# Attention products as tiles of TensorE's array: scores on alternating row groups, po and pi in two halves of their output columns

## The chip, the cores and the metric

One core of one Trainium2 chip runs the program. The metric is the device time of one execution in microseconds (us), lower is better. Engines: PE is TensorE (a matmul is a weight load, listed under PEld, and a streaming part, listed under PE), DVE is VectorE, ACT is ScalarE, POOL is GpSimd, SP issues DMAs.

## The reference, cut to what matters

Three stages in a row: a gated linear attention (a recurrence over 768 steps for each of 4 x 8 heads of size 40), a feed-forward layer, and a layer of 8 experts of which each token takes one.

```python
C = f_stab[:, :, None, None] * C + i_stab[:, :, None, None] * np.einsum('bhd,bhe->bhde', vt, kt)
n = f_stab[:, :, None] * n + i_stab[:, :, None] * kt
h_tilde = np.einsum('bhde,bhe->bhd', C, qt)
nq = np.einsum('bhd,bhd->bh', n, qt)[:, :, None]
y[:, :, t] = o * h_tilde / np.maximum(np.abs(nq), 1.0)
...
h = x @ w_in                 # 3072 x 320 by 320 x 2048
x = (h - np.tanh(h)) @ w_out
...
h = np.maximum(x[mask] @ w1[e], 0.0)
out[mask] = gate_w[mask, None] * (h @ w2[e])
```

## The kernel before, in words

The recurrence is worked in 6 chunks of 128 time steps. A **unit** is one chunk of one batch entry, 8 heads together, so there are 24 units (4 in each chunk). The q and k of a unit lie transposed in SBUF with two heads in one column of 128 partitions: even heads in partitions 0 to 39, odd heads in 64 to 103. All attention matmuls have fp32 operands, and the trace holds two records (a weight load and a matmul each) for one of them.

A unit's work is a list of small functions in `unit`:

- `scores(par)` (S) makes the products of k and q for the four heads of one parity into one PSUM bank `ps`, 4 matmuls with 40 rows of weights, 128 columns of weights and 128 streamed columns (line 517). Then ACT takes the exponentials of the decay tile `D` (line 521) and POOL masks it (line 522).
- `weigh(par)` (W): DVE multiplies `ps` by `D` into `A` (line 533), which frees the bank.
- `outs` (O): `po` is the carried state `Cst` under q, 4 matmuls of 104 x 128 weights and 82 streamed columns (line 541, not in chunk 0); `st`, in the same bank, is the new state, 8 matmuls with 40 columns of weights, at output partitions 0 and 64 in turn (line 545, not in the last chunk); `pi` is `A` times v, 8 matmuls of 128 x 128 weights and 41 streamed columns (line 548).
- `sums`, `finish` (M, F): DVE joins `po` and `pi`, normalises, and updates the state. `turn` (U) transposes the result into `px` (line 597), `low` (L) writes it as the two halves `xh` and `xl` of the feed-forward layer's input (lines 602 and 604).

The feed-forward layer runs in 6 x 16 steps, one for each chunk and each 128 columns of `w_in`. A step issues `gemm1` of three steps ahead (8 matmuls of 512 streamed columns into `h`, line 183), ACT and DVE work on `h` (lines 207 to 216 and 160), and `gemm2` of this step (12 matmuls of 320 streamed columns, lines 191 to 193). It works on chunk c while the attention of chunk c+1 is slotted between its steps: unit b of a chunk has its `scores(0)` in step 4b - 4, counted from the start of the chunk whose layer is being worked, and `scores(1)` one step later. `PLACE1` and `PLACE2` give each function its step offset and its slot, `ORDER` is the order of the slots in a step. The attention of chunk 0 and of the first unit of chunk 1 stands in a list written out by hand, `START`, and goes before. A scheduler may move an instruction ahead of one that stands earlier and isn't ready. After step 96 come the experts (80 steps of the same kind, lines 183 and 191 to 193 again), with no attention beside them.

From `START` on, PSUM banks for the attention come from `at_bank`: in `START` out of 7 banks in turn, later out of the two banks of the pool `at`, which `ps`, `po`, `pi` and `px` share.

Of the kernel before, what the change touches and what calls it, by code (L numbers as in the profile page):

```python
# [21 lines left out]
L = 128  # L22
# [86 lines left out]
def build(ctx, tc, qk, vk, og, gat, w64, w12, emb, tau, cst, tok, empty, out):  # L109
    nc = tc.nc  # L110
    V, A, G, T = nc.vector, nc.scalar, nc.gpsimd, nc.tensor
    MM = T.matmul
# [31 lines left out]
    def at_bank(name):  # L144

        if wide:
            pool, tag = wide[0]
            wide.append(wide.pop(0))
            return pool.tile([128, 512], F32, tag=tag, name=name)
        return at_p.tile([128, 512], F32, tag="at", name=name)  # L150
# [222 lines left out]
    Cst = attp.tile([104, 16, 82], F32, tag="C", name="C", bufs=1)  # L373
# [16 lines left out]
    def load_d(i):  # L390

        if i < NCH * B:
            c, b = divmod(i, B)
            for par in range(2):
                r0 = (8 * b + 4 * par) * L
                src = gd[min(c, 1)][max(c - 1, 0), r0:r0 + 4 * L].partition_broadcast(128)
                if c:
                    t = attp.tile([128, 4, L], F32, tag="D", name="D", bufs=4)
                else:
                    t = wpool.tile([128, 4, L], F32, tag="wi", name="D")  # L400
                nc.sync.dma_start(out=t.rearrange("p h t -> p (h t)"), in_=src)
                Dg[i, par] = t
# [7 lines left out]
    def load_unit(i, early=False):  # L410

        if early:
            a = []
            for tag, src in (("wi", qk[i, :, 0:512]), ("wi", qk[i, :, 512:1024]), ("wo", vk[i, :, 0:328]), ("wo", vk[i, :, 328:648])):
                t = wpool.tile([128, src.shape[1]], F32, tag=tag, name="ue")
                nc.sync.dma_start(out=t, in_=src)
                a.append(t)
        else:
            t = attp.tile([128, 1024], F32, tag="W", name="W")
            nc.sync.dma_start(out=t, in_=qk[i])  # L420
            a = [t[:, 0:512], t[:, 512:1024]] + load_vk(i)
        units[i] = a
# [75 lines left out]
    def attention(c):  # L498
# [3 lines left out]
        def unit(b):  # L502
            i = c * B + b
            uq, uk, uv, ukk = units.pop(i)
            qT = uq.rearrange("p (j t) -> p j t", j=4)
            kT = uk.rearrange("p (j t) -> p j t", j=4)
            v1 = uv.rearrange("p (h d) -> p h d", h=8)
            kk = ukk.rearrange("p (h d) -> p h d", h=8)
            v = {}

            def scores(par):
                p0 = 64 * par
                ps = v['ps', par] = at_bank("ps")
                warm(ps)
                for j in range(4):
                    sl = slice(j * L, (j + 1) * L)
                    MM(ps[:, sl], kT[p0:p0 + 40, j, :], qT[p0:p0 + 40, j, :], start=True, stop=True)
                Dt = v['D', par] = Dg.pop((i, par))
                for j in range(4):
                    k = 8 * i + 4 * par + j  # L520
                    A.activation(out=Dt[:, j, :], in_=Dt[:, j, :], func=AF.Exp, bias=bcol[:, k:k + 1])  # L521
                G.affine_select(out=Dt, in_=Dt, pattern=[[0, 4], [1, L]], compare_op=ALU.is_ge, fill=0.0,  # L522
                                base=0, channel_multiplier=-1)
# [12 lines left out]
            def outs():  # L536
                po = v['po'] = at_bank("po")
                st = po[:, 336:500].rearrange("p (j d) -> p j d", j=4)
                if c:
                    for j in range(4):  # L540
                        MM(po[:, 82 * j:82 * j + 82], qT[0:104, j, :], Cst[:, 4 * b + j, :], start=True, stop=True)
                if c + 1 < NCH:
                    for h in range(8):
                        p0 = 64 * (h % 2)
                        MM(st[p0:p0 + 40, h // 2, :], v['kw'][:, h, :], v1[:, h, :], start=True, stop=True)
                pi = v['pi'] = at_bank("pi")
                for h in range(8):
                    MM(pi[:, 41 * h:41 * h + 41], v['A', h % 2][:, h // 2, :], v1[:, h, :], start=True, stop=True)
                if i >= 4:
                    load_d(i + 2)  # L550
                if 4 <= i < NCH * B - 2:
                    load_unit(i + 2)
# [46 lines left out]
            def low():  # L599
# [7 lines left out]
                nc.sync.dma_start(out=ys[i * 128:(i + 1) * 128, :], in_=v['y'][:, 0:320])  # L607

            return scores, weigh, outs, sums, finish, turn, low

        us = {}
# [113 lines left out]
    def warm(bank, n=None):  # L725
        for _ in range((WARM if c0[0] else 0) if n is None else n):
            MM(bank, oneb, busy, start=True, stop=True)
# [146 lines left out]
    def step(n):  # L874

        if n < NS:
            return n // NF, n % NF, None
        p, f = divmod(n - NS, NFE)
        return p, f, PASSES[p]
# [56 lines left out]
    for n in range(NS + NE):  # L936
        c, f, ps = step(n)
# [73 lines left out]
    def first(w, xt):  # L1011
        h = at_bank("h")
        for k in range(3):
            n = min(128, 320 - 128 * k)
            MM(h[:, 0:128], w[0:n, 128 * k:128 * k + 128], xt[0:n, k, :], start=k == 0, stop=k == 2)
        return h
# [6 lines left out]
    with tc.If(reg > CAP):  # L1023
# [5 lines left out]
        with tc.If(reg > 4096):  # L1029
# [7 lines left out]
            with tc.For_i(0, NT, 128) as i:  # L1037
# [4 lines left out]
                with tc.For_i(0, DFF, 128) as f:  # L1042
# [10 lines left out]
                    h = first(wf, xt)[:, 0:128]  # L1053
# [27 lines left out]
        for e in range(E):  # L1081
            tiles = nc.values_load(nti[0:1, e:e + 1], min_val=0, max_val=NT // 128)
            V.tensor_copy(out=off, in_=st[:, e:e + 1])
            with tc.For_i(0, tiles):
# [11 lines left out]
                for f in range(NFE):  # L1096
                    nc.sync.dma_start(out=wf, in_=w12[e * NFE + f])
                    h = first(wf, xt)[:, 0:128]
# [70 lines left out]
```

## Time and profile before

| | |
|---|---|
| median of 3 runs | 798.19 us (793.8, 798.33, 798.19) |
| the profiled execution | 794.33 us, its span 792.6 us |
| mean granted clock of TensorE | 0.959 |
| PE, PEld busy | 756.1 us (95%), 672.6 us (85%) |
| DVE, ACT, POOL busy | 572.8 us (72%), 448.9 us (57%), 175.2 us (22%) |
| DMA | 98.51 MB, mean 124 GB/s |

The span is the time from the first to the last instruction; 1.7 us of the execution lie outside it. Busy times are of the whole span, and the stages have different limits, so the shares are read by stage. A row of the timeline merges neighbouring instructions of one kind: "x8" is eight of them, the time beside it is from the first one's start to the last one's end, and a matmul's end is modelled.

### The profile page before, as it was taken

To read this page: it belongs to the slowest core of one execution; us is meant where nothing else is said; L and a number is where in the kernel's file an instruction comes from. 1 tells how busy PE (TensorE), PEld (TensorE's weight loads), DVE (VectorE), ACT (ScalarE), POOL (GpSimd) and SP (SyncE) were. 2 spreads that over 40 slices of the span, in tenths; PEclk is the share of its full clock that TensorE was granted. 3 is DMA by queue.
4 is the path that set the end of the run, shared out by engine and by line. 5 is a ranking of instruction groups with operands and counts; after the bars stand their busy time and mean duration, and the time that the engine had idled before them with its cause. 6 is when DMAs were issued, how large, how long until landed. Compare 5 with 4: busy or idle time off the path is not lost. (4 is left out here: it accounts for less than half of the span.)

```text
span 792.6 us, 13944 instructions
## 1 busy us (share of the span) xinstructions
PE 756.1 (95%) x4768; PEld 672.6 (85%) x4768; DVE 572.8 (72%) x1464; ACT 448.9 (57%) x1079; POOL 175.2 (22%) x231
## 2 busy tenths in 40 slices
PE   8979998999999999999999999798999999999993
PEld 4758787788888888888888888687999999999993
DVE  5385899889886988699768877995747765556310
ACT  3686687684457555754567445765636645546321
POOL 2292265411131112111211011302031102102111
PEclk8557999999999999999999999999999999999998
DMA  7665777522242223322251102014265745535000
GB/s 253 230 202 214 257 255 262 160 81 76 69 149 77 79 71 112 112 79 79 70 153 50 40 34 91 1 55 149 98 209 152 226 148 172 146 126 164 25 22 22
DMA packets 47281, 98.51 MB, mean 124 GB/s; under 512 B 13278, under 2 KB 21641, under 8 KB 46544
## 3 DMA queue, kind: packets, MB, share of 16 engines
q1 hardware_dynamic: 44496, 89.44, 35.6%
q0 software_dynamic: 2512, 7.89, 2.6%
q8 instruction: 39, 0.64, 0.3%
q14 instruction: 42, 0.34, 0.1%
q10 hardware_dynamic: 192, 0.20, 0.1%
HBM read 85.57 MB, written 17.87 MB: 131 GB/s over the span
## 5 line engine op out<-in xcount | busy, mean ns | idle before, releaser
L183 PE MATMUL h<-xh,wi 128*128 128x512 f32 (+6 forms) x880 | 295.0, 372 | 6.8 <-ACT xh L847 2.6
L191 PE MATMUL acc<-wo,ghi 128*128 128x320 f32 (+1 forms) x616 | 197.4, 321 | 6.1 <-ACT ghi L215 4.2
L183 PEld LDWEIGHTS h<-xh,wi 128*128 128x128 f32 x880 | 164.6, 190 | 33.7 <-DVE glo L160 4.5
L183 PE MATMUL h<-xl,wi 128*128 128x512 f32 (+6 forms) x528 | 190.9, 366 | 0.0
L192 PE MATMUL acc<-wo,ghi 128*128 128x320 f32 (+1 forms) x616 | 190.5, 310 | 0.0
L193 PE MATMUL acc<-wo,glo 128*128 128x320 f32 (+1 forms) x616 | 185.4, 311 | 0.0
L191 PEld LDWEIGHTS acc<-wo,ghi 128*128 128x128 f32 (+1 forms) x616 | 114.7, 186 | 11.6 <-ACT ghi L215 6.9
L192 PEld LDWEIGHTS acc<-wo,ghi 128*128 128x128 f32 (+1 forms) x616 | 114.7, 186 | 2.8
L193 PEld LDWEIGHTS acc<-wo,glo 128*128 128x128 f32 (+1 forms) x616 | 113.3, 185 | 2.5
L183 PEld LDWEIGHTS h<-xl,wi 128*128 128x128 f32 x528 | 100.7, 191 | 10.0
L215 ACT ACTIVATE ghi<-h 128x512 fp32r<-128x512 f32 x96 | 56.8, 591 | 76.0 <-DVE h L210 42.7
L207 ACT ACTIVATE u<-h 128x512 f32<-128x512 f32 x96 | 57.1, 595 | 72.8 <-PE h L183 70.3
L870 DVE SCALAR_TENSOR_TENSOR glo<-h,ghi 128x256 fp32r<-128x256 f32 (+5 forms) x80 | 41.4, 517 | 60.6 <-ACT ghi L869 53.7
L521 ACT ACTIVATE D<-D,bcol 128x128 f32<-128x128 f32 x192 | 63.5, 391 | 32.3 <-DMA D<-gd 28.5
L209 DVE SCALAR_TENSOR_TENSOR s<-s,u 128x512 f32<-128x512 f32 x96 | 69.4, 723 | 16.2 <-ACT s L208 15.6
L522 POOL TENSOR_SCALAR_AFFINE_SELECT D<-D 128x512 f32<-128x512 f32 x48 | 34.5, 719 | 209.3 <-ACT D L521 158.0
L160 DVE TENSOR_TENSOR glo<-h,ghi 128x512 fp32r<-128x512 f32 x96 | 66.1, 689 | 19.0 <-ACT ghi L215 14.9
L260 DVE SCALAR_TENSOR_TENSOR jk<-R,enb 128x320 bf16<-128x320 f32 x152 | 77.1, 508 | 3.0 <-ACT R L668 2.8
L869 ACT ACTIVATE ghi<-h 128x256 fp32r<-128x256 f32 (+5 forms) x80 | 36.7, 459 | 66.9 <-PE acc L192 59.7
L208 ACT ACTIVATE s<-u,cs 128x512 f32<-128x512 f32 x96 | 69.2, 721 | 1.1
L160 DVE TENSOR_TENSOR wi<-ew,wi 128x256 fp32r<-128x256 f32 (+1 forms) x128 | 46.1, 360 | 28.7 <-ACT wi L172 27.3
L210 DVE SCALAR_TENSOR_TENSOR h<-s,h 128x512 f32<-128x512 f32 x96 | 66.1, 689 | 0.6
(180 smaller groups left out, 1017.4 us busy)
## 6 DMA issues: line engine op xcount, KB each, us to landing
ew<-in_w SPq DMA_DIRECT2D x64, 352.0 KB
D<-gd SPq DMA_DIRECT2D x48, 256.0 KB
raw<-in_w SPq DMA_DIRECT2D x16, 704.0 KB
W<-in_qk SPq DMA_DIRECT2D x20, 512.0 KB
vk<-in_vk SPq DMA_DIRECT2D x20, 324.0 KB
xs<-blank SPq DMA_DIRECT2D x32, 161.0 KB
sg<-in_og SPq DMA_DIRECT2D x6, 640.0 KB
ys<-y SPq DMA_DIRECT2D x24, 160.0 KB
```

Of the source, the lines that this page charges most:

```text
L160: eng.tensor_tensor(out=out, in0=x, in1=hi.bitcast(F32), op=ALU.subtract)
L183: MM(h[:, 0:cols], wi[:, k, :], x[:, kk, :], start=n == 0, stop=n == len(seq) - 1)
L191: MM(o, ghi[:, sl], wo[:, 0, 0:320], start=first, stop=False)
L192: MM(o, ghi[:, sl], wo[:, 1, 0:320], start=False, stop=False)
L193: MM(o, glo[:, sl], wo[:, 0, 0:320], start=False, stop=last)
L207: A.activation(out=u, in_=h, func=AF.Square, accum_out=usum[:, n:n + 1])
L208: A.activation(out=s, in_=u, func=AF.Square, bias=col(C_BETA))
L209: V.scalar_tensor_tensor(out=s, in0=s, scalar=GAMMA, in1=u, op0=ALU.add, op1=ALU.mult)
L210: V.scalar_tensor_tensor(out=h, in0=s, scalar=C2, in1=h, op0=ALU.mult, op1=ALU.mult)
L215: A.activation(out=ghi, in_=g, func=AF.Copy)
L260: V.scalar_tensor_tensor(out=jk[1], in0=x2, scalar=1.0, in1=enb[:, e, :], op0=ALU.mult, op1=ALU.mult, accum_out=lg[:, j, e:e + 1])
L521: A.activation(out=Dt[:, j, :], in_=Dt[:, j, :], func=AF.Exp, bias=bcol[:, k:k + 1])
```

## The change

`scores(0)` now makes the matmuls of both parities: it takes two banks, and goes over j with the even head (partitions 0 to 39) into one bank and the odd head (partitions 64 to 103) into the other in turn. `scores(1)` keeps only its exponentials and mask. Each matmul for `po` and for `pi` becomes two, with columns 0 to 63 and 64 to 127 of the weights, which write output partitions 0 to 63 and 64 to 127; each streams the same 82 or 41 columns as before. `st` stays as it is.

```diff
             def scores(par):
-                p0 = 64 * par
-                ps = v['ps', par] = at_bank("ps")
-                warm(ps)
-                for j in range(4):
-                    sl = slice(j * L, (j + 1) * L)
-                    MM(ps[:, sl], kT[p0:p0 + 40, j, :], qT[p0:p0 + 40, j, :], start=True, stop=True)
+                if par == 0:
+                    for p in range(2):
+                        v['ps', p] = at_bank("ps")
+                        warm(v['ps', p])
+                    for j in range(4):
+                        sl = slice(j * L, (j + 1) * L)
+                        for p in range(2):
+                            r = slice(64 * p, 64 * p + 40)
+                            MM(v['ps', p][:, sl], kT[r, j, :], qT[r, j, :], start=True, stop=True)
...
                 if c:
                     for j in range(4):
-                        MM(po[:, 82 * j:82 * j + 82], qT[0:104, j, :], Cst[:, 4 * b + j, :], start=True, stop=True)
+                        for p0 in (0, 64):
+                            MM(po[p0:p0 + 64, 82 * j:82 * j + 82], qT[0:104, j, p0:p0 + 64], Cst[:, 4 * b + j, :],
+                               start=True, stop=True)
...
                 for h in range(8):
-                    MM(pi[:, 41 * h:41 * h + 41], v['A', h % 2][:, h // 2, :], v1[:, h, :], start=True, stop=True)
+                    for p0 in (0, 64):
+                        MM(pi[p0:p0 + 64, 41 * h:41 * h + 41], v['A', h % 2][:, h // 2, p0:p0 + 64], v1[:, h, :],
+                           start=True, stop=True)
```

## Rows read from the trace of the kernel before

**Rows 1.** Busy time by stage: length, then busy us (instructions) of each engine, clock.

```profile
14.00:38.00 24.00, 23.97 (x124) 18.85 (x124) 7.40 (x13) 13.40 (x31) 5.66 (x11) 0.50 0.79 284
38.00:60.00 22.00, 16.06 (x93) 12.87 (x91) 19.92 (x39) 18.26 (x45) 20.62 (x25) 0.50 0.61 192
72.23:155.00 82.77, 76.13 (x471) 63.97 (x470) 75.09 (x129) 57.09 (x137) 38.86 (x46) 0.96 0.65 213
155.00:486.00 331.00, 331.00 (x2173) 293.08 (x2173) 273.37 (x783) 190.65 (x453) 51.08 (x68) 1.00 0.27 85
486.00:792.00 306.00, 285.69 (x1811) 269.03 (x1809) 181.20 (x468) 156.04 (x381) 51.43 (x67) 0.99 0.37 114
```

**Rows 2.** PE's timeline around one unit's `outs` and the next unit's scores: start, length.

```profile
202.63 0.31 PE L193 MATMUL acc<-wo,glo 128*128 128x320 f32 x1
202.78 1.02 PE L541 MATMUL po<-C,W 104*128 104x82 f32 x8
203.59 0.48 PE L183 MATMUL h<-xh,wi 128*128 128x512 f32 x1
203.90 0.39 PE L183 MATMUL h<-xl,wi 128*128 128x512 f32 x1
...
205.63 0.51 PE L545 MATMUL po<-vk,kw 128*40 128x41 f32 x16
206.07 1.98 PE L548 MATMUL pi<-vk,A 128*128 128x41 f32 x16
207.87 0.40 PE L191 MATMUL acc<-wo,ghi 128*128 128x320 f32 x1
...
213.22 0.31 PE L193 MATMUL acc<-wo,glo 128*128 128x320 f32 x1
213.46 1.16 PE L517 MATMUL ps<-W 40*128 40x128 f32 x8
214.54 0.50 PE L183 MATMUL h<-xh,wi 128*128 128x512 f32 x1
214.88 0.40 PE L183 MATMUL h<-xl,wi 128*128 128x512 f32 x1
```

**Rows 3.** PE's timeline of a step without attention beside it.

```profile
485.27 0.31 PE L193 MATMUL acc<-wo,glo 128*128 128x320 f32 x1
485.41 0.40 PE L183 MATMUL h<-xh,wi 128*128 128x512 f32 x1
485.65 0.40 PE L183 MATMUL h<-xl,wi 128*128 128x512 f32 x1
...
489.05 0.40 PE L183 MATMUL h<-xh,wi 128*128 128x512 f32 x1
```

**Rows 4.** Weight loads by line and shape: count, busy us, mean ns of one.

```profile
L548 PEld LDWEIGHTS pi<-vk,A 128*128 128x128 f32 x320 | 37.5, 191 | 1.4 <-DVE A L533 0.4
L545 PEld LDWEIGHTS po<-vk,kw 128*40 128x40 f32 x256 | 6.5, 118 | 2.8 <-issue 1.3 <-DVE kw L531 0.3
```

**Rows 5.** PE's timeline in the last chunk's attention, where `st` is missing.

```profile
410.58 1.02 PE L541 MATMUL po<-C,W 104*128 104x82 f32 x8
411.44 1.92 PE L548 MATMUL pi<-vk,A 128*128 128x41 f32 x16
413.18 0.39 PE L191 MATMUL acc<-wo,ghi 128*128 128x320 f32 x1
```

**Rows 6.** The four quarters of one chunk, one unit in each: columns as in rows 1.

```profile
253.23:273.93 20.70, 20.70 (x141) 18.40 (x140) 19.47 (x62) 11.83 (x32) 3.25 (x5) 1.00 0.25 76
273.93:294.69 20.76, 20.76 (x141) 18.28 (x140) 19.07 (x57) 9.85 (x24) 2.86 (x5) 1.00 0.23 75
294.69:315.60 20.91, 20.91 (x142) 18.44 (x141) 16.41 (x52) 10.91 (x27) 6.31 (x8) 1.00 0.30 90
315.60:336.30 20.70, 20.70 (x140) 18.41 (x139) 13.60 (x28) 15.62 (x34) 3.74 (x6) 1.00 0.41 125
```

**Rows 7.** Timeline of DVE and PE where a chunk's last unit ends: banks, and `glo` before `gemm2`.

```profile
234.38 1.16 PE L517 MATMUL ps<-W 40*128 40x128 f32 x8
235.62 0.69 DVE L533 TENSOR_TENSOR A<-ps,D 128x512 f32<-128x512 f32 x1
...
237.43 0.49 PE L597 MATMUL px<-cs,y 128*128 128x128 f32 x3
...
239.61 1.16 PE L517 MATMUL ps<-W 40*128 40x128 f32 x8
...
240.85 0.69 DVE L533 TENSOR_TENSOR A<-ps,D 128x512 f32<-128x512 f32 x1 [0.98 <-PE ps L517]
...
245.97 0.69 DVE L160 TENSOR_TENSOR glo<-h,ghi 128x512 fp32r<-128x512 f32 x1 [0.16 <-ACT ghi L215]
...
247.63 0.39 PE L191 MATMUL acc<-wo,ghi 128*128 128x320 f32 x1
```

**Rows 8.** Timeline of ACT and DVE in the hand-ordered start: what DVE waits for.

```profile
31.75 1.27 ACT L435 ACTIVATE sg<-sg 128x1280 f32<-128x1280 f32 x1 [6.85 <-DMA sg<-in_og]
...
38.03 0.69 DVE L533 TENSOR_TENSOR A<-ps,D 128x512 f32<-128x512 f32 x1 [9.23 <-POOL D L522]
```

## The prediction

> **What bounds the kernel now.** I read the busy times by stage first, then PE's timeline inside the stage that matters, then the other engines there. From 155 to 486 us, which holds the attention of chunks 2 to 5 (16 units) beside the feed-forward layer, PE is busy for all 331.00 us and never waits [rows 1]. A busy PE may still be a slow one, so the reader must see what one record costs. A step without attention lasts 3.64 us, from 485.41 to 489.05 [rows 3]. A quarter of a chunk, four steps and one unit, lasts 20.7 us [rows 6]; less 4 x 3.64 = 14.6 that leaves 6.1 us for a unit's attention, all of it PE time in a stage that waits for nothing else. DVE is second with 273.37 of 331 us.
>
> The other stages are not PE's alone. From 72 to 155 us (chunk 1's attention) DVE is busy for 75.09 of 82.77 us, and PE waits for 6.6. From 14 to 38 us PE is busy at half clock, but DVE waits 9.23 us there for the decay tile, and that goes back to ACT, which waited 6.85 us for a transfer [rows 8]: PE's matmuls aren't what is late. From 38 to 60 us DVE, ACT and POOL are each busy for 18 to 21 of 22 us. After 486 us nothing is changed.
>
> **What a record costs.** `pi` has 16 records in 1.80 us (206.07 to 207.87), 112 ns each; `po` has 8, and from the last matmul before it to the second one of `h` 1.27 us pass (202.63 to 203.90) where a step without it has 0.38 (485.27 to 485.65): 0.89 us, 111 ns each [rows 2, 3]. Records with 41 and with 82 streamed columns cost the same, so it is the load of 128 columns of weights that sets the pace, not the stream. `st` is the precedent for the change: 40 columns of weights, the same 41 streamed, output partitions 0 and 64 in turn, and 16 records take at most 0.44 us (205.63 to 206.07), 27 ns each [rows 2]. A load of 40 columns at pi's pace would alone take 112 x 40 / 128 = 35 ns, so two loads on different column groups must have run at once.
>
> **pi in halves.** 16 records become 32 of 64 columns. At 56 ns a load (half of 112) and two at once, 16 x 56 = 0.90 us instead of 1.80: 0.90 us gained. Bounds: if the halves don't overlap, 32 x 56 = 1.79, nothing gained; if each record goes on costing 112 ns, 1.8 us lost. I take the overlap, as `st` is the nearest row by far: same engine mode, same stream, same alternation.
>
> **po in halves.** 8 records become 16 with 82 streamed columns each. Two loads at once give 8 x 56 = 0.45 us. The stream may bound it instead: `st`'s pair of records, with 41 columns, took up to 55 ns, so 82 columns may take up to 110, and then nothing is gained. I take 73 ns, the middle between 56 and 90 rounded to the low side, because the 27 ns hold `st`'s start and end as well: 8 x 73 = 0.58 us, 0.31 gained, bounds 0 to 0.44.
>
> **Changing the shape of the array.** A run of scores costs 214.88 - 213.22 = 1.66 us less 0.38, so 1.28 us, while its 8 records at 112 ns are 0.89 [rows 2, 3]. The other 0.39 us are the way in and out: the first load is no longer hidden, nor is the first one of `h` behind it. The Trainium skill, TensorEngine Tiling (Array Packing), section Key Properties, says that a change of the tiling mode, though not of the tile, drains the engine; by that rule the halves, though they make nothing else worse, cost every run of `po` and `pi` that had no such change its 0.39 us, which the trace bears out for the scores and for no other run; if it were not so, the last chunk would gain 1.6 us more. Where `po`, `st` and `pi` follow one another they already hold one such change (for `st`). Where `po` stands alone, with `h` between, as at 202.78, it gets a change of its own: 3 of the 12 units of chunks 2 to 4. In the last chunk there is no `st`, and `po` and `pi` now run undisturbed [rows 5], so each of its 4 units pays 0.39 us anew.
>
> **Scores.** Two runs become one of 16 records, so one way in and out, 0.39 us, goes. If loads and streams of the two row groups run at once, into two banks, the 16 records take the time of 8 and the whole run costs 1.28 us instead of 2.56: 1.28 gained. If they don't, 0.39 is gained. No row shows alternating row groups; `st` shows it for column groups, and I take the upper value for the same reason.
>
> **The two banks.** `ps` of the odd heads is now held from the even heads' run until its `weigh`, one step longer: about 6 us (235 to 241.5) instead of 1.9 [rows 7]. Between lies the transpose `px` of the unit before, which needs the other bank, so it stands behind `weigh(0)`. That is over at 236.31, and `px` began at 237.43, so 1.1 us cover it; the even heads end at most 0.9 us later than now. If the cover goes, `px`, the `gemm2` behind it in PE's queue and `low` wait about 1 us in a unit, 16 us in all. I cost it at nothing. `po` and `pi` come 3 us after the second `weigh`. ACT's and POOL's work, the DMA issues and their order stay.
>
> **The sum.** Chunks 2 to 4: 12 x (1.28 + 0.90 + 0.31) = 29.9, less 3 x 0.39 = 1.2. Chunk 5: 4 x (2.49 - 0.39) = 8.4. Together 37.1 us.
>
> What comes next? DVE is busy for 38.5 us in the first two quarters [rows 6]. They would take PE 41.5 - 5.0 = 36.5. So DVE falls 2 us behind there, and catches up in the other two (30.0 of 41.6). At the chunk's end only 1.0 us lie between `glo` (done at 246.66) and the `gemm2` that reads it at 247.63 [rows 7], after ACT's sigmoid; 2.5 us less in this quarter makes that a wait of about 1.5. I give back 1.5 us a chunk, 6 us, with bounds of 0 and 12. That leaves 31.
>
> Chunk 1's attention: its units lose 4 x 2.49 = 10 us of PE work, but PE has 6.6 us of waits and DVE 91%; I take 3, bounds 0 and 8. Start: 1, bounds 0 and 3. In sum 35 us off the profiled execution: 794.3 - 35 = 759. With every bound at its worse end it is 25 us, 769, with every one at its better end 48, 746; all the better ends at once are unlikely, and I let this case reach from 752 to 769. Two of the three runs before took 4 us more than that execution, one 0.5 less; I put the median of the changed kernel at 761, between 759 and 763.
>
> **Rivals.**
> *Row groups don't overlap.* No row shows that they do. The scores then gain 0.39 instead of 1.28: 16 x 0.89 = 14 us less, 773 to 777.
> *PE can't be fed faster.* `st` is the longest dense run, 16 records; `po`, `st` and `pi` now make 64 in one go. If PE takes a record every X ns in a long run, a unit gains 2.56 - 0.39 + 0.89 + 1.80 - 64X, which is 0.88 at X = 62 and nothing at X = 76. With X = 56 `pi` and `po` gain nothing and the scores all: 16 x 1.28 = 20 us, less 2.8 for the changes of shape, with 2 from chunk 1: 20, so 774; with X = 65, 16 x 0.7 = 11 on the same terms: 10, so 784. For it: 112 ns is the pace of every longer run. Against: `st` at 27. The Trainium skill, TensorE: Matmul & The Clock Gate, section "Wait — 56ns, not 53.3ns?", has about 62 ns for a matmul that the sequencer must decode by program, and 25 ns as the floor otherwise; by the first a unit would gain 0.9 us and the kernel would come to 780 or so. `st` agrees with the second, as far as its 16 records reach.
> *Slower: a record costs the same whatever its width.* If the chip keeps to 112 ns a record in `po` and `pi`, and only the scores' way in and out is saved, 20 units lose 1.80 + 0.89 - 0.39 = 2.3 us: 46 us, 840. It decides from X = 76 on. Against it stand `st`'s row and its loads, 118 ns on average against pi's 191 for 128 columns [rows 4].
> *Hidden anyway.* DVE binds from 72 us on. For it: it is over 90% busy in half of every chunk. Against: 82% in the stage. Its floor there is 273 us, so at least part of the 37 us must show; with 15 us left, 780.
>
> **How the numbers follow.** Overlap in all parts 0.60 (752 to 769); row groups without overlap 0.17; fed too slowly 0.10; hidden by DVE 0.06; slower, or a wait for banks that costs more than is gained, 0.07. The range of 752 to 781 takes in the first two and about half of the next two, 0.85, and leaves out the tail. About 1% (8 us) is what a measurement of this kernel can tell from no change, so faster by over 1% means below 790: 0.60 + 0.17 + 0.09 + 0.03 = 0.89; same 0.05, slower 0.06.
>
> **What would show it.** In PE's timeline of 155 to 486 us a unit has one run of `ps` with 16 records in 1.2 to 1.3 us (2.1 if row groups don't overlap); `pi` 32 records in about 0.9 us (1.8 or more if not); `po` 16 in about 0.6. The quarters of a chunk last 18.2 to 18.6 us, PE still without waits in most of them, and the chunk's first half DVE's at 95% or more. The rest, from the end of the attention on, keeps its 306 us. The prediction is wrong if the quarters get shorter by less than the runs do (then the waits name the engine), if `px` waits for DVE's `A`, or if the clock's share in this stage falls below 1.00.

## The result and the profile after

The changed kernel takes 767.38 us (median of 4 runs, 767.0 to 771.64), the kernel before 796.0 beside it (4 runs): a ratio of 0.966, 95% interval 0.960 to 0.971. Its profiled execution took 767.0 us, the span 765.2, against 794.33 and 792.6: 27.3 us less, where the sum had said 35.

First the busy times by stage, in the columns of [rows 1]; the stages end where the same work ends.

```profile
14.00:38.00 24.00, 14.38 (x160) 11.06 (x162) 8.29 (x15) 13.86 (x32) 6.26 (x11) 0.62 0.78 291
38.00:59.00 21.00, 10.15 (x113) 7.38 (x113) 18.42 (x36) 16.99 (x42) 19.85 (x24) 0.50 0.64 210
70.48:150.60 80.12, 72.67 (x553) 58.99 (x549) 73.81 (x128) 57.93 (x137) 37.27 (x45) 0.94 0.67 223
150.60:460.50 309.90, 304.96 (x2564) 262.78 (x2565) 273.35 (x787) 190.51 (x453) 56.85 (x70) 1.00 0.29 92
```

The stage of chunks 2 to 5 went from 331.00 to 309.90 us. DVE works there as long as before (273.35 against 273.37 us), PE 26 us less. But PE, which never waited, now has 5 us without work. From 14 to 59 us PE works 24.5 us, where it was 40.0 from 14 to 60 (part of it is the clock, 0.62 instead of 0.50 up to 38 us), and only 1 to 2 us are gained there.

PE's timeline of one unit's products and the next unit's scores, against [rows 2]:

```profile
218.54 0.63 PE L183 MATMUL h<-xh,wi 128*128 128x512 f32 x2
219.10 0.79 PE L545 MATMUL po<-C,W 104*64 104x82 f32 x16
219.72 0.48 PE L550 MATMUL po<-vk,kw 128*40 128x41 f32 x16
220.02 1.11 PE L554 MATMUL pi<-vk,A 128*64 128x41 f32 x32
221.06 0.41 PE L191 MATMUL acc<-wo,ghi 128*128 128x320 f32 x1
221.31 0.31 PE L192 MATMUL acc<-wo,ghi 128*128 128x320 f32 x1
...
226.41 0.31 PE L193 MATMUL acc<-wo,glo 128*128 128x320 f32 x1
226.65 1.16 PE L520 MATMUL ps<-W 40*128 40x128 f32 x16
227.74 0.50 PE L183 MATMUL h<-xh,wi 128*128 128x512 f32 x1
228.09 0.40 PE L183 MATMUL h<-xl,wi 128*128 128x512 f32 x1
```

Read start to start, since ends are modelled. The 16 records of scores take 1.09 us, as long as 8 did. From the last `gemm2` to the second record of `h` it is 228.09 - 226.41 = 1.68 us, 1.30 above a step without scores; the prediction had 1.28. `pi` takes 1.04 us for 32 records where 16 took 1.80. For `po`, `st` and `pi` in one go the same place of another unit of before is the measure:

```profile
225.64 1.02 PE L541 MATMUL po<-C,W 104*128 104x82 f32 x8
...
228.82 0.39 PE L191 MATMUL acc<-wo,ghi 128*128 128x320 f32 x1
229.06 0.30 PE L192 MATMUL acc<-wo,ghi 128*128 128x320 f32 x1
```

That is 3.18 us, now 221.06 - 219.10 = 1.96. The last chunk, against [rows 5]: 450.32 - 448.68 = 1.64 us for what took 2.60.

```profile
448.68 0.79 PE L545 MATMUL po<-C,W 104*64 104x82 f32 x16
...
450.32 0.41 PE L191 MATMUL acc<-wo,ghi 128*128 128x320 f32 x1
```

So each run got about as much shorter as forecast. The quarters of the same chunk as in [rows 6] did not:

```profile
244.71:263.85 19.14, 18.86 (x164) 16.33 (x163) 18.59 (x57) 11.33 (x30) 3.75 (x4) 1.00 0.25 82
263.85:283.78 19.93, 19.07 (x164) 16.28 (x163) 18.88 (x58) 10.20 (x25) 3.25 (x5) 1.00 0.24 79
283.78:303.09 19.31, 19.15 (x167) 16.39 (x166) 17.43 (x53) 10.61 (x26) 6.57 (x8) 1.00 0.32 99
303.09:322.47 19.38, 19.16 (x164) 16.22 (x163) 13.52 (x30) 15.74 (x36) 3.40 (x6) 1.00 0.46 131
```

77.76 us instead of 83.07, 5.3 gained in a chunk. The waits of PE's weight loads from 150 to 461 us (us in all, times, longest) name what took the rest:

```profile
PEld po L545 <- issue: 5.3, 16, 0.4
PEld px L604 <- DVE A L536: 4.1, 6, 1.2
PEld h L183 <- DVE glo L160: 2.3, 6, 1.0
PEld L293 <- DVE oh L286: 1.6, 2, 1.3
```

In the same view of before, from 155 to 486 us, no wait for `A` or `oh`, and none of `h` for `glo`, appears. The first row is no wait for another engine. It is the way into the new shape of `po`: the first load no longer runs beside the last matmul of `h`, so the loads stand for 0.33 us, of which PE itself loses 0.09 (worked out below).

Two of these waits in the timeline. `px` needs a bank, and since the scores fill both banks in one go it has to wait until `A` frees the first one. `A` was late because DVE had other work: from the scores' end at 169.1 us to 171.20 it has no gap, and POOL's mask was ready at 169.92.

```profile
167.94 1.16 PE L520 MATMUL ps<-W 40*128 40x128 f32 x16
...
171.20 0.68 DVE L536 TENSOR_TENSOR A<-ps,D 128x512 f32<-128x512 f32 x1
171.94 0.55 PE L604 MATMUL px<-cs,y 128*128 128x128 f32 x3 [0.77 <-DVE A L536]
```

And `gemm1` stands in PE's queue in the middle of `pi` and waits for one of the two banks of `h`, which `glo` of two steps earlier has to free; the rest of `pi` waits behind it:

```profile
236.72 0.52 PE L554 MATMUL pi<-vk,A 128*64 128x41 f32 x10
237.34 0.69 DVE L160 TENSOR_TENSOR glo<-h,ghi 128x512 fp32r<-128x512 f32 x1 [0.80 <-ACT ghi L215]
238.09 0.50 PE L183 MATMUL h<-xh,wi 128*128 128x512 f32 x1 [0.85 <-DVE glo L160]
```

Of the six waits of `px` for `A` five, with 3.9 of the 4.1 us, lie in the first two quarters of a chunk, where DVE is busy 97% and 95% of the time.

The start stands where [rows 8] had it, and DVE's `A` comes 0.3 us earlier: ACT waits 5.88 us for a transfer, DVE 9.12 for the decay tile.

```profile
37.72 0.69 DVE L536 TENSOR_TENSOR A<-ps,D 128x512 f32<-128x512 f32 x1 [9.12 <-POOL D L525]
```

A yardstick for the experiments: the time from the first `gemm2` record of step 16 to that of step 79, 63 steps with 15 units. Before it lasts 320.2 us (170.7 to 490.9), after 299.3 (166.1 to 465.4). In the tables below the time of a product is summed from each of its records to the next matmul's start in this stretch, so it includes waits in front of what follows.

### The profile page after: what moved, and what is told of

Same layout as the page of the kernel before. It is cut to its first block, busy times and chain, and to the rows that moved or that the text cites. A ratio compares the mean times of both kernels' runs of the same rounds, so it can differ in the third digit from the quotient of the medians.

```text
span 765.2 us, 15047 instructions
## 1 busy us (share of the span) xinstructions
PE 708.6 (93%) x5310; PEld 622.4 (81%) x5312; DVE 570.8 (75%) x1464; ACT 448.9 (59%) x1079; POOL 180.5 (24%) x231
## 5 line engine op out<-in xcount | busy, mean ns | idle before, releaser
L183 PEld LDWEIGHTS h<-xh,wi 128*128 128x128 f32 x880 | 165.3, 191 | 34.3 <-DVE glo L160 7.1
L525 POOL TENSOR_SCALAR_AFFINE_SELECT D<-D 128x512 f32<-128x512 f32 x48 | 36.9, 770 | 179.7 <-ACT D L524 109.8
L160 DVE TENSOR_TENSOR wi<-ew,wi 128x256 fp32r<-128x256 f32 (+1 forms) x128 | 46.2, 361 | 27.8 <-ACT wi L172 26.7
```

The lines of the kernel that those rows point to most:

```text
L160: eng.tensor_tensor(out=out, in0=x, in1=hi.bitcast(F32), op=ALU.subtract)
L183: MM(h[:, 0:cols], wi[:, k, :], x[:, kk, :], start=n == 0, stop=n == len(seq) - 1)
```

## The experiments

The theory after the result: the runs are as short as forecast, and what is missing is waits that the shorter runs uncover. Its forms differ in what is waited for: DVE as a whole, the banks of `h`, or the banks of `at`. The rival is that PE itself can't be fed in long runs.

**One part at a time.** Each is the kernel before with one hunk of the diff.

> Scores alternate as in the changed kernel, po and pi as before. Theory: the scores' gain of 1.28 us a unit (16 units) shows almost whole, since DVE is further from its limit than with all three parts: 18 to 22 us faster than before, about 774 us, one run of 16 records in 1.1 us, and px waits for DVE's A in few units. Rival (the two banks held longer cost what is missing): px or po wait in most units and only 10 to 14 us are gained, 781 us.

> Only pi is made in halves. Theory: 32 records in about 1.0 us for 16 in 1.8, 0.75 us a unit in 16 units plus 1 to 3 us before them: 13 to 16 us faster, about 780 us. If the parts are simply additive in time, scores alone, pi alone and po alone sum to the 27 to 29 us of the whole change; if DVE gives part of it back, they sum to 35 or more.

> Only po is made in halves. Theory: a run of po falls from 0.81 us to 0.62, but it needs a change of the array's shape of its own (0.3 to 0.4 us) wherever it doesn't stand beside st, and pi is again in full width behind it: between 2 us faster and 5 us slower, 790 to 797 us. Rival (the po halves gain 0.31 us a unit as forecast): 4 to 5 us faster.

| | median us | ratio, 95% | step 16 starts at | steps 16 to 79 | `ps` | `pi` | `po` |
|---|---|---|---|---|---|---|---|
| before | 795.98 | | 170.7 | 320.2 | 32.3 | 26.9 | 13.4 |
| scores alone | 782.42 | 0.982, 0.976 to 0.989 | 166.2 | 312.2 | 21.0 | 26.7 | 13.6 |
| `pi` alone | 779.36 | 0.981, 0.974 to 0.988 | 163.6 | 310.7 | 32.8 | 16.2 | 14.0 |
| `po` alone | 791.87 | 0.995, 0.992 to 0.998 | 170.2 | 318.5 | 32.3 | 26.9 | 10.2 |
| all three | 767.38 | 0.966, 0.960 to 0.971 | 166.1 | 299.3 | 17.8 | 17.2 | 11.0 |

Every part pays, `pi` most. The sum is 13.6 + 16.6 + 4.1 = 34.3 us, together they bring 28.6. The intervals of the single gains are 2 to 6 us wide to either side, so this difference isn't shown; and what there is of it lies ahead of step 16, which comes 4.5, 7.1 and 0.5 us earlier with one part and 4.6 with all three. In the stretch the gains add up: 8.0 + 9.5 + 1.7 = 19.2 us, together 20.9. So what is given back there isn't lost where the parts meet, it is lost by the single parts already.

Most of it by the scores. Alone they came out at their rival's price (781), though not by its waits (`px` for `A` costs 0.9 us): the stretch gives 8.0 us where 15 units at 1.28 are 19.2 (9.9 without the one `gemm1` more, 512 records against 504, that falls into it). In 6 of the 15 units the second bank came late, and the run stands in two pieces or takes longer: `ps` costs 21.0 us where 15 runs of 1.09 are 16.4. `po` alone came out as its rival had it, `pi` alone as expected or a little better.

**The overlap of the row groups taken away.** The changed kernel with the four even heads first and then the four odd ones, in the same step and the same two banks.

```diff
-                    for j in range(4):
-                        sl = slice(j * L, (j + 1) * L)
-                        for p in range(2):
-                            r = slice(64 * p, 64 * p + 40)
+                    for p in range(2):
+                        r = slice(64 * p, 64 * p + 40)
+                        for j in range(4):
+                            sl = slice(j * L, (j + 1) * L)
```

> As the changed kernel, but the scores make the four even heads first and then the four odd ones, in the same step and the same two banks. Theory (the gain is the overlap of the two row groups): the run is 1.8 to 2.0 us instead of 1.1, about 0.85 us a unit more, less what DVE would have taken back: 8 to 14 us slower than the changed kernel, 775 to 781 us. Rival (the gain is one way in and out instead of two): the run stays near 1.1 us and the time at 767.

769.41 us (ratio 0.966, 0.960 to 0.972). Its run of scores in PE's timeline:

```profile
224.92 1.71 PE L520 MATMUL ps<-W 40*128 40x128 f32 x16
226.56 0.50 PE L183 MATMUL h<-xh,wi 128*128 128x512 f32 x1
```

1.64 us instead of 1.09: alternating does make two row groups run at once, 59 ns a record within the run instead of 96. The overlap isn't gone altogether: in the middle of the run three pairs of records still start 4 to 5 ns apart (at 225.47, 225.69 and 225.80), much as all pairs do in the changed kernel, and the others, but for the first, follow at 106 to 112 ns. That is why the run is shorter than the 1.8 to 2.0 us expected. Over 15 units `ps` costs 26.0 us instead of 17.8. But the stretch is only 3.2 us longer, and the whole kernel 2 us, which these runs can't tell from nothing; neither expectation came out whole. `h` takes 3.6 us less than in the changed kernel (122.0 against 125.6), and PE's own waits of `px` for `A` and of `h` for `glo` shrink from 1.9 and 1.1 us to 0.4 and 0.2. So of the 8.2 us that the overlap frees in `ps` 3.2 arrive, and 2.4 of the rest are these two waits.

**The order of pi's halves.** All first halves, then all second ones.

```diff
-                for h in range(8):
-                    for p0 in (0, 64):
+                for p0 in (0, 64):
+                    for h in range(8):
```

> The changed kernel with pi's halves in another order: all eight first halves, then all eight second halves, so that neighbours use the same column group. Theory (two column groups load at once only if neighbours alternate): 32 records at 56 ns, a run of 1.8 us instead of 1.0, 0.75 us a unit or less as DVE has time to catch up: 4 to 12 us slower than the changed kernel, 771 to 779 us. Rival (narrow weights are cheap by themselves): no change.

781.85 us (0.983, 0.980 to 0.986), slower than either side expected; `pi` costs 29.1 us in the stretch, 11.9 more than with alternation.

```profile
179.64 1.72 PE L554 MATMUL pi<-vk,A 128*64 128x41 f32 x30
181.28 0.42 PE L191 MATMUL acc<-wo,ghi 128*128 128x320 f32 x1
```

30 records in 1.49 us from first to last, 51 ns each on average. In the middle, where first and second halves meet, some still alternate; neighbours of one half follow each other at 58 ns (179.64 to 180.22 us), about half of the 112 ns of full width, so a load's time does follow its columns. Alternation halves it once more, to 28 ns. The rival "the same whatever its width" falls, and the gain of `pi` is the alternation's alone: grouped halves cost 29.1 us where the full width cost 26.9 (two of the runs hold pauses, of which below).

**DVE relieved.** In chunks 1 to 3 two of the router's eight dot products for a token block go from DVE to POOL and ACT, in the kernel after and in the one before. (Their intermediate takes a buffer of `A`'s pool.)

```diff
-VDOT = (8, 8, 8, 8, 6, 0)
+VDOT = (8, 6, 6, 6, 6, 0)
```

> The changed kernel with a quarter of the routing's dot products taken from DVE in chunks 1 to 3 as well: POOL multiplies and ACT sums (two of eight experts' products for each row tile, 8 products of 0.5 us, 4 us of DVE time a chunk). Theory (DVE's first half of a chunk takes back what PE gained): 1 to 2 us a chunk faster than the changed kernel, 3 to 6 us in all, about 763 us. Rival (the wait is for PSUM banks, not for DVE's load): no change, 767 us, or a little slower by ACT's and POOL's added work.

> The same move of dot products in the kernel before, as a control. Both theories: PE waits for nothing from 155 to 486 us there, so the time stays within 1 us of 796, or gets a little slower.

The changed kernel gets slower, 779.85 us (0.981, 0.978 to 0.984), well above both times expected; the one before stays, 795.56 (0.999, 0.996 to 1.003). In the third quarter (284 to 304 us) DVE is now busy for 14.36 of 20.00 us, and PE waits more, not less. Its longest wait from 150 to 470 us, and what stands behind it:

```profile
PE h L183 <- DVE glo L160: 8.5, 10, 1.7
DVE glo L160 <- ACT ghi L215: 15.1, 16, 3.2
ACT jk L265 <- POOL dt L264: 10.8, 14, 1.4
```

`glo` waits for ACT's `ghi` 15.1 us, against 8.0 in the changed kernel, and ACT stands for 10.8 us before its new sums until POOL has the products. So work moved to ACT stands in the way of the chain from `h` to `glo`. Whether DVE's load binds is not settled by this: from 244 to 264 us, in the first quarter, DVE is as full as ever (19.87 of 20.00 us).

**The bank of h freed earlier.** The last DVE operation of the chain writes a tile in SBUF and not its bank, so `gemm1` two steps later need not wait for `glo`; again in both kernels.

```diff
-        V.scalar_tensor_tensor(out=h, in0=s, scalar=C2, in1=h, op0=ALU.mult, op1=ALU.mult)
-        return h
+        V.scalar_tensor_tensor(out=u, in0=s, scalar=C2, in1=h, op0=ALU.mult, op1=ALU.mult)
+        return u
```

> The changed kernel, but the last DVE operation of the layer's chain writes its result to the SBUF tile u instead of back into the PSUM bank of h, so that the bank is free before ghi and glo are made, some 1.5 to 2.5 us earlier. Theory (PE now waits because gemm1 of three steps ahead needs one of two h banks, which is freed only when glo two steps earlier is done): the waits of h for glo vanish, 3 to 6 us faster than the changed kernel, about 763 us. Rival (the loss is DVE's total load): DVE has as much to do, so no change, 767 us.

> The same edit in the kernel before, as a control. First theory: the h bank is free in time there (0.4 us or more to spare in every step from 171 to 486 us), so nothing is gained in that stage; at most 1 to 3 us elsewhere, where PE waits already (72 to 155 us, 494 to 535 us): 793 to 796 us. Rival: the same gain as in the changed kernel, 3 to 6 us, would say that the wait is none of the change's doing.

The kernel before gains little, 791.62 us (0.997, 0.994 to 0.999), and nothing in the stretch (320.6 us). The changed one gets slower, 777.32 (0.979, 0.975 to 0.982), outside both times expected. It is 4.9 us ahead at step 16 (161.2 against 166.1) and loses 15.1 in the stretch (314.4). The wait for `glo` is gone, and others are there:

```profile
PE px L604 <- DVE A L536: 6.5, 7, 1.3
PE pi L554 <- issue: 4.1, 10, 0.5
```

So freeing the bank of `h` is not enough by itself: with it free, the scheduler orders the rest otherwise, and `px` waits for `A`. The second row is new. In PE's timeline:

```profile
297.33 0.47 PE L550 MATMUL po<-vk,kw 128*40 128x41 f32 x16
297.63 0.69 PE L554 MATMUL pi<-vk,A 128*64 128x41 f32 x17
298.54 0.33 PE L554 MATMUL pi<-vk,A 128*64 128x41 f32 x3 [0.22 <-issue]
299.30 0.35 PE L554 MATMUL pi<-vk,A 128*64 128x41 f32 x4 [0.43 <-issue]
```

After some 50 records at 28 ns PE takes a few, pauses for 0.4 us with no wait that the profile shows, takes a few more: 4 us for a `pi` that takes 1.04 elsewhere. That looks like the rival "PE can't be fed", at single places.

**The scores behind px.** The scores' place is moved behind `px`'s, `weigh` to the next step, so that `px` need not wait for `A`.

```diff
-PLACE2 = {'S': (0, 7), 'W': (0, 1), 'O': (3, 5), 'M': (3, 6), 'F': (4, 5), 'U': (4, 2), 'L': (4, 2)}
+PLACE2 = {'S': (0, 0), 'W': (1, 3), 'O': (3, 5), 'M': (3, 6), 'F': (4, 5), 'U': (4, 2), 'L': (4, 2)}
```

> The changed kernel with the scores of chunks 2 to 5 put behind the transpose of the unit before, and the weighing into the first slot of the next step, so that px takes its bank before the two score banks are taken. Theory that DVE's load is what is missing: px no longer waits for A, but the waits of h for glo stay, and the scores now wait for px's bank: within 2 us of the changed kernel, 765 to 769 us. Rival (the banks held longer are what is missing): 4 to 8 us faster, 760 us, and PE's waits fall to nearly nothing.

790.2 us (0.993, 0.991 to 0.995), far outside both times expected. `px` now holds one of the two banks, so the scores find only one and run as two times 8 records of 1.085 us: `ps` costs 32.7 us, as before the change, and the same pauses stand in `pi` (3.8 us). `h` hardly waits (121.2 us). Of the gain of the scores nothing is left when their two banks aren't free together.

**po back at full width,** in the changed kernel and in the one with `h` freed earlier; the run of `po`, `st` and `pi` is then 56 records and not 64.

```diff
-                        for p0 in (0, 64):
-                            MM(po[p0:p0 + 64, 82 * j:82 * j + 82], qT[0:104, j, p0:p0 + 64], Cst[:, 4 * b + j, :],
-                               start=True, stop=True)
+                        MM(po[:, 82 * j:82 * j + 82], qT[0:104, j, :], Cst[:, 4 * b + j, :], start=True, stop=True)
```

> The changed kernel with po back at its full width (8 records); scores and pi stay changed. If gains of the single parts add up, the 4.1 us that the po part alone brought are lost: 771 to 772 us. If the halves of po cost elsewhere what they save in their own run (a change of the array's shape in the units where po stands alone, 64 records in one go instead of 56), it is 764 to 768, the same as the changed kernel or a little better.

> The kernel after_u (the last DVE operation of the feed-forward chain writes SBUF instead of the PSUM bank h) with po back at its full width. If PE's stalls inside pi (about 0.5 us each after some 45 to 56 quick records in a row) come from the length of the dense run, they vanish with 8 records fewer, and the time is 765 to 772 us. If they come from what the schedule puts around it (pi waiting for A or for its bank), they stay, and the time is 775 to 780, near the 777.3 of after_u.

779.58 us (0.980, 0.976 to 0.983) and 778.19 (0.980, 0.976 to 0.983). The first lies outside both times expected: without the halves of `po` the changed kernel loses 12.2 us, not 4.1. `po` itself costs 4.9 us more in the stretch; the rest is waiting, in the same view as for the changed kernel above:

```profile
PEld h L183 <- DVE glo L160: 5.8, 9, 1.4
PEld px L602 <- DVE A L536: 5.7, 9, 1.1
PEld h L183 <- ACT xh L607: 2.3, 3, 1.0
PEld L293 <- DVE oh L286: 1.6, 3, 1.0
```

15.4 us against 8.4 (the wait for `xh` is 0.4 there); 7.0 + 4.9 = 11.9, about the 11.4 us by which the stretch is longer (310.7). So what an edit of a third of a microsecond in a unit does to the order of the queues weighs more here than the edit. The second came out as its rival had it: the pauses in `pi` are fewer but not gone (1.86 and 1.76 us from first to last record in two of its runs), so the length of the run alone doesn't make them.

## Why the prediction was right, and where it was off

761 was forecast, 767.4 measured, within the range. The likeliest case came true in its runs; what is given back it had too small, and two of the three signs that it named for being wrong appeared: the quarters got shorter by less than the runs did (19.1 to 19.9 us, where 18.2 to 18.6 were foreseen), and `px` waits for DVE's `A`.

- *Scores:* 1.28 us a unit forecast. Before, two runs of 1.28; now one of 1.30, so 1.26 gained. Alternating row groups do run at once, which no row had shown; the argument from `st`'s column groups held.
- *po, st and pi:* 1.21 us forecast (0.90 + 0.31). 3.18 us became 1.96; less 0.09 for the way in (0.327 instead of 0.233 us between the last record of `h` and `po`) and 0.02 for the way out (the first record of `gemm2` behind `pi` takes 0.252 us, and took 0.231 before), 1.11 gained. A pair of halves takes 65 ns in `pi` and not 56, and 78 in `po` and not 73.
- *Change of shape:* 0.39 us was charged where nothing hid it; for `po` and `pi` alone in the last chunk it is 0.11. There 0.82 was forecast, and 2.60 - 1.64 - 0.11 = 0.85 came. That `st` holds one change already was right. The rule of the Trainium skill (TensorEngine Tiling (Array Packing), section Key Properties) that a change of mode drains the engine agrees with the trace on the way in, at less than a third of the price that was put on it.
- *The sum of PE's work* is thus right: for the 15 units of the stretch 11 x 2.49 + 4 x 2.10 - 1.2 = 34.6 forecast, 11 x (1.26 + 1.11) + 4 x (1.26 + 0.85) = 34.5 if every run were like the ones shown. That the two come so near is in part luck: `po` and `pi` gained less than forecast, and the changes of shape cost less.
- *The give-back is the term that was mis-sized.* 20.9 of these 34.5 us arrive (320.2 - 299.3): 13.6 are given back, where 6 stood, with a bound of 12. By record, the products got 27.6 us shorter in the stretch (`ps` 14.5, `pi` 9.7, `po` 2.4, `st` 1.0), and `h`, `gemm2` and `px`, whose work is the same, 6.7 longer. What the runs show for it: the loads' waits above, `px` for `A` 4.1, `gemm1` for a bank of `h` 2.3, the router for `oh` 1.6, together 8.0 (PE itself is without work for 4.9 us in the whole stage). About 1.5 are scores not in one go because the second bank came late (at 207.00 they take 1.79 us, at 285.63 1.29; one run is cut in two at 397.09 and 401.32). In 6 of the 12 units of chunks 2 to 4, not 3, records of `h` stand within or right behind `po`, in two more within `pi`, in one of the last chunk within `po`: a way in and out more each. These overlap in part, and the rest I can't place.
- *Its reason* was half right. DVE's first two quarters do cost PE time, but not at the place that was named: `gemm2` at the chunk's end waiting for `glo` doesn't show in the waits, `px` waiting for `A` does.
- *The two banks* were costed at nothing, and that step failed. The cover of 1.1 us [rows 7] was read at the last unit of a chunk. At the other units of before there was little or none; the rows at the end of this list show one where `px` starts before `A` is done. From 195 to 404 us, `px` starts 1.1 us behind `A`'s end in the 3 last units of a chunk and between 0.6 us before and 0.3 behind it in the 8 others. So the trace of before could have told that `px` would wait: now it does in 6 of the stretch's units, for 4.1 us. The 16 us of the worst case didn't come, though moving the scores behind `px` shows that they can.
- *Up to step 16:* 3 for chunk 1, 1 for the start and one unit, 2.5, were forecast; 170.7 - 166.1 = 4.6 came. After step 79 another 1.9 us are gone, which nothing in the change accounts for; from there to the end the 14 kernels traced take 299.8 to 303.1 us.
- *The range:* its worse end of 25 us was to take every bound, but `po`'s own bound of 0 (16 x 0.31 = 5 us) isn't in it. It wasn't needed.
- *The rivals:* row groups overlap (59 ns against 96). A record's price follows its width (58 and 28 ns against 112). PE is fed fast enough in the changed kernel, not in all its neighbours. With 28 ns a record in `pi`, the trace does not bear out the 62 ns of the Trainium skill (TensorE: Matmul & The Clock Gate, section "Wait — 56ns, not 53.3ns?"). It goes below the floor of 25 ns given there too: `st` has 16 records from 219.72 to 220.02, 19 ns each. "Hidden by DVE" is half true: the first two quarters are 97% and 95% DVE's, as forecast, and that is where `px` waits; the run that was to relieve DVE doesn't settle what a DVE with less to do would give. The clock kept 1.00 in the stage.

```profile
299.52 0.68 DVE L533 TENSOR_TENSOR A<-ps,D 128x512 f32<-128x512 f32 x1
299.60 0.38 PE L597 MATMUL px<-cs,y 128*128 128x128 f32 x2
```

Not settled is whether an order of the queues exists that keeps the 13.6 us. Each wait that was taken away here (the bank of `h`, the bank for `px`) brought up another, since the scheduler reorders everything behind it; no version tried beats the changed kernel.

## What to carry to other kernels

Small products gained here from being spread over the array's row or column groups where neighbouring instructions alternated between the groups and the output banks that they need were free at the same moment; grouped halves of `pi` brought nothing. Sum the runs first, which came out to within a microsecond or two here, and then ask of every tile with two buffers how much slack it had, at each place where it is used and not at the most favourable one: at a bottleneck that gets shorter these slacks become the waits. Where a scheduler orders the queues, an edit's own price can be the smaller part of what it does, so judge it with the others in place.

## What the runs showed of the hardware that was not expected

The pauses inside `pi` come at a certain time. Over all 14 kernels traced there are 35 places from 150 to 470 us where over 0.3 us lie between the starts of two neighbouring records of these runs. All of them are in `pi`, and all lie within 2.3 us of the start of one of POOL's four scatters of a chunk, although only about a quarter of all such records do. They stand in 15 runs of `pi`, at most one in a chunk, so whatever else recurs at that place of a chunk coincides as well. The kernel with `po` at full width:

```profile
305.05 1.22 PE L552 MATMUL pi<-vk,A 128*64 128x41 f32 x31
305.26 0.97 POOL L154 DMA_INDIRECT xs<-R,si  x1 [0.30 <-issue]
306.63 0.20 PE L552 MATMUL pi<-vk,A 128*64 128x41 f32 x1 [0.36 <-issue]
```

In the kernels whose `pi` has full width (112 ns a record) there is none, and none either in three with halves: `pi` alone, the even heads first, and the changed kernel, whose `pi` at 298.31 lies among scatters as well. During 32 of the 35 no transfer of the queues that carry instructions is under way, so a late one isn't seen either. A run without scatters wasn't made, so this is a coincidence in time and not a cause shown; what PE lacks in these pauses stays open.
